# One fused attention and feed-forward kernel: the order of every engine's queue is made anew, and some operations change engine

## The chip, the cores and the metric

The kernel runs on one core of one Trainium2 chip. A time is the device time of one execution in microseconds (us). The profile shows one execution: its span is the time from the first to the last instruction that the hardware profiler recorded. The engines are named as in the profile: PE (TensorE, with PEld for its weight loads), DVE (VectorE), ACT (ScalarE), POOL (GpSimd) and SP (SyncE, which here only issues transfers). L12 is line 12 of the kernel.

## The reference

The program first computes a routed attention and then a feed-forward layer on its result. Tokens attend only to tokens of the same cluster; the cluster is the centroid that lies nearest by angle.

```python
q_assign = np.argmax(np.einsum('bhsd,hcd->bhsc', q_n, c_n), axis=-1)
k_assign = np.argmax(np.einsum('bhsd,hcd->bhsc', k_n, c_n), axis=-1)
mask = q_assign[:, :, :, None] == k_assign[:, :, None, :]
scores = np.where(mask, scale * np.matmul(q, k.transpose(0, 1, 3, 2)), -1e9)
attn = np.exp(scores - np.max(scores, axis=-1, keepdims=True))
x = np.matmul(attn / (np.sum(attn, axis=-1, keepdims=True) + 1e-09), v)
# then, on tokens x (head, dim):
h = x @ w_in
solu = h * softmax(h)
out = ((solu - mean(solu)) / sqrt(var(solu) + 1e-06) * g_ln) @ w_out
```

There are 4 batches of 8 heads with 768 tokens of 64 numbers, 16 centroids for each head, and a feed-forward layer from 512 to 1024 to 512 over the 3072 tokens. All inputs and the output are float32.

## The kernel before

**Work and stages.** Heads are taken in pairs, 16 pairs in all (batch.pair, as in 0.3). For each pair, queries and keys are loaded (ld on SP), turned so that the head's dimension lies on the partitions, and cast to bf16 into a tile qk. In batch 0 the turning is done on PE (tp, L391 and L395) with copies out of PSUM (xa, L405, on ACT or DVE); in the other batches it is a transpose on DVE (xt, L419). The casts are called ca (L443 on ACT, L445 for queries and L447 for keys on POOL or DVE). The cluster of each token comes from a matmul against the centroids (cl, L457 or L462), a transpose back on DVE (tb, L471), a maximum over 16 columns (mx, L484), a comparison with it that makes a one-hot row (oh, L489), another transpose (ot, L495), and four copies of it beside the queries and keys (pl, L507 or L514, on POOL or DVE, or as a transfer, L512). A small memset (bl, L523) blanks the columns that belong to the other head. With the one-hot rows beside the data, one matmul gives scores that are shifted down wherever two clusters differ.

**Attention.** The scores of a pair go through PSUM banks of 512 columns: matmuls S (L593), the exponential E on ACT (L599), and the matmuls V (L616) that multiply by the values. The PSUM tile for the scores has 3 buffers, the exponentials have 9, the sums have one. N (L628 and L641, on DVE) divides by the denominators and writes x; the next group's V must wait for it. The values come by lv (SP) and a cast cv (L532).

**Feed-forward.** Tokens go in 24 blocks f of 128. For each there is a transposing transfer of x (tx, SP, L671; the last block on PE), matmuls h (L702), the maximum hm on DVE (L708), the exponential ex on ACT (L714), the product u on DVE (L721), a transposing transfer tu (SP, L726), statistics bn and ag on DVE (L732, L736), the scale factor at and al on POOL (L742 to L751), the output matmuls y (L768) and the scaling sc (L786 on ACT, L788 on DVE), and the store ou. h of the block after next, and part of the next, writes into the PSUM bank that u of block f has read. The output weights are loaded (lo), summed (su, L571, DVE), averaged by one matmul (me) and centred (ce, L579, DVE); the input weights are loaded (li) and cast (wi, L551, POOL).

**What sets the order.** Each of these operations is registered under its name. A table ORDER holds one string for each engine: it lists kinds of operations, and the k-th entry of a kind takes the k-th registered operation of that kind on that engine. A table AWAY names the operations that leave their usual engine. An engine works through its instructions in this order and stops at one whose inputs are not there. The tables were written out by a search ahead of time; the kernel itself does no search.

## Time and profile before

| what | value |
| --- | --- |
| median of 3 runs | 228.95 us (228.57 to 230.77) |
| the profiled execution, its own time | 228.39 us |
| its span | 226.4 us |
| PE busy | 218.4 us, 96% |
| DVE busy | 200.4 us, 89%, 353 instructions |
| ACT busy | 194.7 us, 86%, 378 instructions |
| POOL busy | 132.9 us, 59%, 256 instructions |
| moved by DMA | 39.00 MB, mean 172 GB/s |

The profiled execution took 2.0 us more than its span, and lies 0.56 us below the median. A busy share is an average over stages: the first 60 us are attention alone with all preparations of the first batch and of the weights, from about 55 to 205 us attention and feed-forward run side by side, and the last 20 us are feed-forward alone. An engine's row in the profile gives busy time, number of instructions and mean duration of one; instructions of one engine can overlap a little, so a sum of durations is more than the engine's busy time.

### The profile page before, as it was taken

To read this page: it belongs to the slowest core of one execution; us is meant where nothing else is said; L and a number is where in the kernel's file an instruction comes from. 1 tells how busy PE (TensorE), PEld (TensorE's weight loads), DVE (VectorE), ACT (ScalarE), POOL (GpSimd) and SP (SyncE) were. 2 spreads that over 40 slices of the span, in tenths; PEclk is the share of its full clock that TensorE was granted. 3 is DMA by queue.
4 is the path that set the end of the run, shared out by engine and by line. 5 is a ranking of instruction groups with operands and counts; after the bars stand their busy time and mean duration, and the time that the engine had idled before them with its cause. 6 is when DMAs were issued, how large, how long until landed. Compare 5 with 4: busy or idle time off the path is not lost.

```text
span 226.4 us, 6687 instructions
## 1 busy us (share of the span) xinstructions
PE 218.4 (96%) x2460; PEld 148.7 (66%) x2460; DVE 200.4 (89%) x353; ACT 194.7 (86%) x378; POOL 132.9 (59%) x256
## 2 busy tenths in 40 slices
PE   7899988999999999999999999999999999999993
PEld 4566655666777767686577767687677677675452
DVE  3699999999999899999999989899899969798991
ACT  3689979999999999999889999899999999974352
POOL 4577799982498589387949742485908403223311
PEclk9999999999999999999999999999999999999999
DMA  6996988699998999999998949579924441476922
GB/s 154 343 353 163 258 226 120 256 157 252 149 172 147 248 229 181 146 166 163 185 232 144 215 101 210 126 161 210 243 59 110 97 116 26 61 150 181 186 86 106
DMA packets 123183, 39.00 MB, mean 172 GB/s; under 512 B 112008, under 2 KB 117904, under 8 KB 123152
## 3 DMA queue, kind: packets, MB, share of 16 engines
q1 hardware_dynamic: 122432, 38.06, 79.5%
q10 hardware_dynamic: 720, 0.52, 0.8%
q8 instruction: 19, 0.31, 0.6%
q14 instruction: 12, 0.10, 0.1%
HBM read 23.11 MB, written 6.29 MB: 130 GB/s over the span
## 4 chain that ended last, share of the span: by engine, by line
PE 74%; DMA 8%; DVE 8%; SPq 7%; issue 1%; ACT 0%; DVEq 0%
PE sps L593 22%; PE hreg L702 18%; PE yps L768 17%; PE ops L616 13%; SPq L411 4%; PE csc L462 3%; DMA w_g<-in_moe_w_out_dram 3%; DMA w_st<-in_moe_w_in_dram 2%; DVE w_out_c L579 2%; DMA raw<-in_k_dram 2%; DVE xt L419 1%; SPq L564 1%; DMA raw<-in_q_dram 1%; PE hreg L768 1%; SPq L376 1%
## 5 line engine op out<-in xcount | busy, mean ns | idle before, releaser
L599 ACT ACTIVATE e<-sps 128x512 bf16<-128x512 f32 (+1 forms) x294 | 151.8, 595 | 11.9 <-PE sps L593 10.1
L593 PE MATMUL sps<-qk 96*128 96x256 bf16 (+5 forms) x636 | 93.3, 264 | 2.1 <-DVE qk L507 0.6
L593 PEld LDWEIGHTS <-qk 96*128 96x128 bf16 (+1 forms) x636 | 59.5, 121 | 27.1 <-issue 7.6
L616 PEld LDWEIGHTS <-e 128*128 128x128 bf16 x1152 | 49.7, 97 | 12.1 <-issue 3.1
L616 PE MATMUL ops<-v,e 128*128 128x65 bf16 x1152 | 54.2, 193 | 0.6 <-DVE x L641 0.5
L702 PE MATMUL hreg<-w_in_sb,xT 128*128 128x512 bf16 x192 | 52.9, 379 | 0.3 <-DVE w_out_c L579 0.3
L768 PE MATMUL yps<-w_out_c,uT 128*128 128x512 bf16 x184 | 47.4, 378 | 0.0
L514 POOL COPY qk<-oht 32x384 f32<-32x384 f32 (+1 forms) x45 | 22.2, 493 | 19.5 <-DVE oht L495 17.1
L721 DVE TENSOR_TENSOR u<-e_sb,hreg 128x1024 bf16<-128x1024 bf16 (+1 forms) x25 | 29.1, 1169 | 2.8 <-ACT e_sb L714 2.5
L708 DVE TENSOR_REDUCE nmax<-hreg 128x1 f32<-128x1024 f32 x24 | 29.3, 1219 | 2.6 <-PE hreg L702 2.0
L732 DVE BATCH_NORM_STATS2 bs<-u 128x6 f32<-128x512 bf16 x48 | 31.2, 674 | 0.2
L714 ACT ACTIVATE e_sb<-hreg,nmax 128x1024 bf16<-128x1024 f32 x24 | 26.9, 1120 | 3.0 <-DVE nmax L708 2.9
L445 POOL CAST qk<-xt 64x768 bf16<-64x768 f32 (+1 forms) x32 | 26.5, 829 | 4.7 <-ACT xt L405 3.3
L447 POOL TENSOR_SCALAR qk<-xt 64x768 bf16<-64x768 f32 (+1 forms) x31 | 26.8, 864 | 2.2 <-DVE xt L405 0.2
L768 PEld LDWEIGHTS <-uT 128*128 128x128 bf16 x200 | 18.3, 97 | 14.2 <-ACT uT L698 0.5
L702 PEld LDWEIGHTS <-xT 128*128 128x128 bf16 x192 | 17.1, 97 | 10.0 <-DVE w_out_c L579 0.6
L419 DVE STREAM_TRANSPOSE xt<-raw 128x768 f32<-128x768 f32 x24 | 22.8, 958 | 0.0
L742 POOL TENSOR_SCALAR es<-esum 128x1 f32<-128x1 f32 x24 | 5.8, 246 | 27.1 <-ACT e_sb L714 26.5
L748 POOL TENSOR_SCALAR esq<-es,mv 128x1 f32<-128x1 f32 x24 | 8.3, 344 | 21.3 <-DVE mv L736 21.1
L641 DVE TENSOR_TENSOR x<-ops,den 128x256 bf16<-128x256 f32 (+1 forms) x39 | 19.0, 486 | 1.3
L532 POOL CAST v<-vf 128x384 bf16<-128x384 f32 x28 | 14.2, 522 | 5.9 <-DMA vf<-in_v_dram 4.5
L786 ACT ACTIVATE y<-yps,alpha 128x512 f32<-128x512 f32 x17 | 11.7, 690 | 6.6 <-PE yps L768 5.8
(79 smaller groups left out, 178.3 us busy)
## 6 DMA issues: line engine op xcount, KB each, us to landing
vf<-in_v_dram SPq DMA_DIRECT2D x16, 384.0 KB, 4.4
out_dram<-y SPq DMA_DIRECT2D x23, 256.0 KB, 2.7
raw<-in_q_dram SPq DMA_DIRECT2D x50, 96.0 KB, 3.1
raw<-in_k_dram SPq DMA_DIRECT2D x50, 96.0 KB, 3.2
w_g<-in_moe_w_out_dram SPq DMA_DIRECT2D x4, 512.0 KB, 7.2
w_st<-in_moe_w_in_dram SPq DMA_DIRECT2D x4, 512.0 KB, 5.3
raw<-in_q_dram SPq DMA_DIRECT2D x3, 384.0 KB, 6.6
raw<-in_k_dram SPq DMA_DIRECT2D x3, 384.0 KB, 7.0
```

The source lines that it names most:

```text
L419: nc.vector.transpose(xt[:], raws[b, p, i][:].rearrange("p j c -> p (j c)"))
L445: VEC[e].tensor_copy(dst, src)
L447: VEC[e].tensor_scalar(dst, src, scalar1=inv_C, scalar2=1.0, op0=Alu.mult, op1=Alu.mult)
L593: nc.tensor.matmul(sps_[n, k][:, c0:c0 + w], side(b, h // 2, 1, h % 2, keys)[r], side(b, h // 2, 0, h % 2, slice(s0 * P, s0 * P + w))[r])
L599: nc.scalar.activation(es[n, k][:, :w], sps_[n, k][:, :w], Act.Exp, scale=exp_scale, bias=-exp_scale)
L616: nc.tensor.matmul(opss[g][:, s, :VW], es[n, k][:, c0:c0 + P], v1[slot(b, h // 2)][:, h % 2, kt, :VW], start=(kt == 0), stop=(kt == n_t - 1))
L702: uses(nc.tensor.matmul(hreg[:, at(f, f2)[1], :], xTs[f][:, dc, :], w_in_sb[:, dc, f2 * FF2:(f2 + 1) * FF2], start=(dc == 0), stop=(dc == ...
L708: uses(nc.vector.tensor_reduce(ff[f, "nmax"][:], pair_of(f), axis=AXY, op=Alu.max, negate=True), *both(f))
L714: uses(nc.scalar.activation(ff[f, "e"][:], pair_of(f), Act.Exp, bias=ff[f, "nmax"][:], accum_out=ff[f, "esum"][:]), *both(f))
L721: uses(nc.vector.tensor_tensor(ff[f, "u"][:, r], ff[f, "e"][:, r], pair_of(f)[:, r], op=Alu.mult), *both(f)[r])
L732: nc.vector.bn_stats(ff[f, "bs"][:, f2, :], ff[f, "u"][:, f2, :])
L768: ins = nc.tensor.matmul(dst, ff[f, "uT"][:, at(f, f2)[0] * (n_fc // 2) + c, :], w_out_c[:, fc, cols], start=(fc == fcs[0] and part % 2 == ...
```

## The change

Both tables are replaced by new ones. The arithmetic, the tiles, the buffers and the set of operations stay as they were. The search that made the new tables took it as a rule that a DVE operation whose operands all lie in SBUF (it touches no PSUM) and a POOL operation cannot run at the same time; the search before had no such rule. What the tables say of the place of each operation changed nearly everywhere, so only one line of the order and the lists of operations moved to ACT and DVE are shown here.

```diff
     ORDER["DVE"] = """
-        cn cb tb mx oh ot pl3 tb mx oh ot xa2 cf ca2 bl tb mx oh gk ot N pl su xa su tb mx oh xa ot
+        cn cb ca tb mx oh ot pl2 tb mx oh ot pl xa2 cf ca cv pl tb mx xa oh gk ot N ca pl tb su mx
...
-        ca0.0.0.1.1 sc23.0 xa0.0.0.1 xa0.0.1.0 xa0.1.0.0 xa0.1.0.1 xa0.2.0.0 xa0.2.0.1 xa0.2.1.0
-        xa0.2.1.1 xa0.3.0.0
+        ca0.0.0.0.0 ca0.1.1.1 ca0.3.0.0 ca2.3.0.0 sc23.0 tu22.1 xa0.0.0.1 xa0.0.1.0 xa0.1.1.0
+        xa0.1.1.1 xa0.2.0.0 xa0.2.0.1 xa0.2.1.1
     """.split(), "ACT"))
     AWAY.update(dict.fromkeys("""
-        bl0.0.1 bl0.2 bl1.2 bl1.3 bl3.3 ca0.0.1.1.1 ca0.1.0.0 cv3.0.0 cv3.1.0 cv3.3.0 cv3.3.1
-        pl0.0.0.1.1 pl0.1.1.0 pl0.2.0.1 pl0.3.0.0 sc10 sc17 sc19 sc2 sc6 sc9 tu22.0
+        bl1.0 bl2.3 ca0.0.0.1.0 ca0.1.0.1 ca0.2.1.1 ca1.0.0.0 ca1.3.0.0 ca1.3.0.1 ca2.0.0.0
+        ca2.2.0.1 ca2.3.1.0 ca3.0.1.1 ca3.3.0.1 cv0.0.0 cv2.2.0 pl0.0.0.0.1 pl0.0.0.1.1 pl0.0.1.0.1
+        pl0.1.1.1 pl0.2.0.0 sc0 sc10 sc12 sc13 sc19 sc23.1 sc3 sc4 sc8 tu22.0
     """.split(), "DVE"))
```

By engine, these counts change: casts ca, on POOL 63 before and 49 now, on DVE 2 and 11 (one of each half-size), on ACT 3 and 8; scalings sc, on ACT 19 and 16, on DVE 6 and 9; copies xa, on DVE 5 and 7, on ACT 11 and 9; casts cv, on DVE 4 and 2; memsets bl, on DVE 5 and 2; copies tu, on DVE 3 and 2. The copies pl on DVE are 6 in both. The changed file has one line more in the SP table, so that every line number behind it is larger by one: L391 is L392, L445 is L446.

The first place is PE's queue at the program's start, behind the warming matmuls: the transposes tp0.0 of the first pair's four half loads (L391), the centroids' transpose cp (L866) and the first cluster matmuls cl0.0.0 (L462). Before:

```order
L391 MATMUL hreg<-ident_f,raw 64x128 x12
L866 MATMUL cps<-ident_f,c_n 128x128
L391 MATMUL hreg<-ident_f,raw 64x128 x6
L462 MATMUL csc<-xt,c_bd 32x192 x4
L391 MATMUL hreg<-ident_f,raw 64x128 x6
```

Now:

```order
L392 MATMUL hreg<-ident_f,raw 64x128 x12
L867 MATMUL cps<-ident_f,c_n 128x128
L463 MATMUL csc<-xt,c_bd 32x192 x4
L392 MATMUL hreg<-ident_f,raw 64x128 x12
L817 LDWEIGHTS w_out_c
```

The first cluster matmuls now stand ahead of the third group of transposes instead of behind it.

The second place is DVE's queue behind the second cluster assignment: xa (L405), cf (L870), casts ca (L445 and L447), a memset bl (L523) and the assignment of pair 0.1 (L471 to L495). Before:

```order
L405 COPY xt<-hreg 128x384 x2
L870 TENSOR_TENSOR w_out_c<-cps,w_out_c 128x512
L447 TENSOR_SCALAR qk_99<-xt 64x384
L445 CAST qk_100<-xt 64x6x128
L523 MEMSET qk_99 16x192
L471 STREAM_TRANSPOSE cst<-csc 128x384
L484 TENSOR_REDUCE mx<-cst 128x24
L489 TENSOR_TENSOR oh<-cst,mx 128x384
```

Now:

```order
L515 COPY qk_99<-oht 32x2x96
L406 COPY xt<-hreg 128x384 x2
L871 TENSOR_TENSOR w_out_c<-cps,w_out_c 128x512
L446 CAST qk_100<-xt 64x6x128
L533 CAST v_0_105<-vf 128x6x64
L515 COPY qk_99<-oht 32x2x96
L472 STREAM_TRANSPOSE cst<-csc 128x384
L485 TENSOR_REDUCE mx<-cst 128x24
L406 COPY xt<-hreg 128x384
L490 TENSOR_TENSOR oh<-cst,mx 128x384
```

A half-size cast and the memset left this stretch, and a cast of values, two copies pl and one more copy xa came into it.

The third place is DVE's queue around hm of block 4 (the row L708, or L709, below), in the stage where attention and feed-forward run side by side; bn and ag are L732 and L736, xt is L419. Before:

```order
L736 BN_AGGR mv<-bs 128x2
L419 STREAM_TRANSPOSE xt<-raw 128x768
L732 BN_STATS bs<-u 128x6 x2
L736 BN_AGGR mv<-bs 128x2
L788 TENSOR_SCALAR y<-yps,alpha 128x512
L708 TENSOR_REDUCE nmax<-hreg 128x1
L628 RECIPROCAL den<-ops 128x4
```

Now:

```order
L420 STREAM_TRANSPOSE xt<-raw 128x768
L709 TENSOR_REDUCE nmax<-hreg 128x1
L446 CAST qk_100<-xt 64x768
L420 STREAM_TRANSPOSE xt<-raw 128x768
L446 CAST qk_100<-xt 64x768
L733 BN_STATS bs<-u 128x6
L629 RECIPROCAL den<-ops 128x6
L642 TENSOR_TENSOR x<-ops,den 128x6x64
```

Behind hm of block 4 stand two casts of queries that POOL did before, and a transpose between them.

## The prediction

> **What bounds the kernel now.** I read the page first for who is busy and when. In its second part each digit is the busy tenth of one fortieth of the span, 5.7 us.

> ```profile
> span 226.4 us, 6687 instructions
> ...
> PE   7899988999999999999999999999999999999993
> ...
> DVE  3699999999999899999999989899899969798991
> ...
> PE 74%; DMA 8%; DVE 8%; SPq 7%; issue 1%; ACT 0%; DVEq 0%
> ```

> PE is full from the tenth slice to the last but one, and the chain that ended last runs through it for 74% of the span. A new order cannot shorten work on a full engine, so a gain must come from the first 55 us or from the last few. The busy time by stretch shows who limits the beginning; the last two rows are the stage in which attention and feed-forward run side by side.

> ```profile
> core 0: us, PE busy (x) PEld busy (x) DVE busy (x) ACT busy (x) POOL busy (x), PEclk, DMA share, GB/s
> 10.00:20.00 10.00, 9.45 (x100) 6.38 (x98) 9.48 (x20) 8.96 (x24) 7.28 (x14) 1.00 1.02 310
> 20.00:30.00 10.00, 9.85 (x124) 6.20 (x122) 9.85 (x16) 8.61 (x20) 8.43 (x15) 1.00 0.84 213
> 30.00:40.00 10.00, 8.25 (x126) 5.45 (x123) 9.59 (x19) 9.00 (x18) 9.38 (x14) 1.00 0.85 171
> 40.00:50.00 10.00, 9.75 (x129) 6.65 (x126) 9.80 (x20) 9.70 (x21) 9.48 (x16) 1.00 0.90 202
> 50.00:60.00 10.00, 9.66 (x117) 7.00 (x116) 9.73 (x16) 9.36 (x19) 3.99 (x8) 1.00 1.00 212
> ...
> 57.80:117.40 59.60, 59.60 (x695) 42.66 (x694) 56.46 (x95) 57.06 (x110) 42.48 (x77) 1.00 1.01 183
> 117.40:216.00 98.60, 98.56 (x1093) 67.38 (x1091) 88.65 (x149) 84.81 (x160) 46.50 (x93) 1.00 0.70 142
> ```

> From 10 to 60 us DVE is the fullest engine: of 50 us it is idle for 10.00 − 9.48 and so on, 1.55 us in all, while PE misses 3.0 us and ACT 4.4. DVE sets the pace there, up to the maximum hm of block 1 at 57.8 us. Between 57.8 and 117.4 us PE is busy for all 59.60 us, DVE idle for 59.60 − 56.46 = 3.1. Between 117.4 and 216 DVE is idle for 98.60 − 88.65 = 10.0.

> **What a collision costs.** The groups by shape and the durations (least, median, most, in ns) of single lines tell which DVE operations lengthen beside POOL.

> ```profile
> L489 DVE TENSOR_TENSOR oh<-cst,mx x17: 516/698/1267, 8.6 to 168.5; 128x384 bf16<-128x384 f32 x15, 128x192 bf16<-128x192 f32 x2
> L571 DVE SCALAR_TENSOR_TENSOR w_sum<-w_g,g_ln,w_sum x7: 703/741/1193, 21.8 to 39.4; 128x512 f32<-128x512 f32 x7
> L507 DVE COPY qk<-oht x3: 473/881/886, 20.0 to 37.2; 32x384 f32<-32x384 f32 x3
> L732 DVE BATCH_NORM_STATS2 bs<-u x48: 637/679/696, 59.8 to 220.3; 128x6 f32<-128x512 bf16 x48
> L419 DVE STREAM_TRANSPOSE xt<-raw x24: 924/968/978, 27.6 to 156.5; 128x768 f32<-128x768 f32 x24
> ...
> 41.65 1.27 DVE L489 TENSOR_TENSOR oh<-cst,mx 128x384 bf16<-128x384 f32 x1
> ...
> 41.47 2.35 POOL L551 CAST w_in_sb<-w_st 128x1024 bf16<-128x1024 f32 x2
> ...
> 5.00:60.00 55.00, 6.25 (x7) 1.00 0.92 230
> ```

> The longest oh, 1.27 us at 41.65, started beside a cast that POOL had begun at 41.47; alone an oh takes 0.52. The statistics and transposes keep their durations within 60 ns, whatever POOL does. The last row is oh alone before 60 us. So in the first 60 us collisions took 6.25 − 7 × 0.516 = 2.6 us in oh, 7 × (0.837 − 0.703) = 0.9 in su (its mean is in the next rows), 0.88 + 0.89 − 2 × 0.47 = 0.8 in two copies pl, and up to 0.5 in one cast, **4.8 us in all**, on the engine that sets the pace.

> **The change part by part.** Durations for what moves:

> ```profile
> L571 DVE SCALAR_TENSOR_TENSOR w_sum<-w_g,g_ln,w_sum 128x512 f32<-128x512 f32 x7 | 5.9, 837 | 0.0
> L788 DVE TENSOR_SCALAR y<-yps,alpha 128x512 f32<-128x512 f32 x6 | 4.5, 746 | 1.3 <-issue 0.8 <-PE yps L768 0.6
> L405 DVE COPY xt<-hreg 128x384 f32<-128x384 f32 x5 | 2.6, 539 | 0.0
> L523 DVE MEMSET qk<- 16x384 f32 x4 | 1.5, 378 | 0.5
> L532 DVE CAST v<-vf 128x384 bf16<-128x384 f32 x4 | 1.3, 351 | 0.0
> L445 DVE CAST qk<-xt 64x768 bf16<-64x768 f32 x1 | 1.1, 1077 | 0.0
> L443 ACT ACTIVATE qk<-xt 64x384 bf16<-64x384 f32 x3 | 1.5, 517 | 0.0
> L405 ACT COPY xt<-hreg 128x384 f32<-128x384 f32 x11 | 5.2, 507 | 3.0 <-PE hreg L391 3.0
> ```

> A full cast on DVE is measured once, 1.08 us, beside POOL. Below, it cannot be less than the cast of half as many columns, 0.35; twice that is 0.70 with the fixed part counted double. I take 0.60 undisturbed and keep 0.35 and 1.08 as ends.

> Start. DVE waits 1.60 us for the first cluster matmuls:

> ```profile
> 5.85 0.29 DVE L876 TENSOR_TENSOR c_bd<-cps,own 128x128 f32<-128x128 f32 x1 [0.71 <-PE cps L866]
> 7.75 0.38 DVE L471 STREAM_TRANSPOSE cst<-csc 128x192 f32<-128x192 f32 x1 [1.60 <-PE csc L462]
> ...
> 6.35 0.87 PE L391 MATMUL hreg<-ident_f,raw 128*64 128x128 f32 x10 [0.17 <-DMA raw<-in_q_dram]
> 7.15 0.53 PE L462 MATMUL csc<-xt,c_bd 128*32 128x192 f32 x8
> ```

> They now stand ahead of the transposes that run from 6.35 with a wait for a load; the wait shortens by some 0.9 us. The half-size cast set ahead of it on DVE (0.5) fits into the 0.7 us left: **−0.9 us**.

> Collisions up to 57.8 us. I take two thirds as avoided, **−3.2**: POOL is rid of 14 casts and the order keeps the pairs apart, but the engines drift against a plan, and every collision avoided must hold on the chip. Ends: 0 and −4.8.

> DVE's added work up to hm of block 1: by the order's rows, two full casts (1.2), two copies xa (1.1), a cast of values (0.35) and less memset (−0.2): **+2.4** (1.9 with casts at 0.35, 3.4 at 1.08). ACT, with 4.4 us idle in this stage, gets two full casts (at most twice 0.52 each) and two half-size ones and gives up two copies xa, +2.1 us, and stays below DVE. Loads hardly shift the limit: the last input weights come behind the same set of transfers, though lo2 and lo3, which feed su, come behind eight small loads now; su5 to su7 stand later on DVE, too.

> Side by side, 57.8 to 117.4 us. DVE gets four full casts (2.4), a cast of values (0.35), two scalings sc (1.5) and two memsets less (−0.8): +3.5 us, against 3.1 of idle time. That idle time is made of waits for h and ex within the loop of a block (h, hm, ex, u, then the next h into the bank), so I count half as usable, 1.6, and 0.5 of collisions of oh gone: **+1.4**. Ends: 0, if all of it is usable; 3.5 or more, if none. PE has no idle time here, so what DVE is late, PE loses for good.

> From 117.4 to 216 us three more casts (1.8) stand against four casts of values fewer (−1.4), with 10 us idle: 0.

> Tail. The chain of the end runs through u, the statistics, DVE's copy of u and the last output matmuls:

> ```profile
> 219.80 1.21 DVE bs L732 x2
> ...
> 221.58 1.50 PE hreg L768 x12
> ...
> 218.67 0.69 ACT L786 ACTIVATE y<-yps,alpha 128x512 f32<-128x512 f32 x1 [0.19 <-POOL esq L748]
> 220.14 0.59 ACT L698 COPY uT<-utp 128x512 bf16<-128x512 bf16 x1 [0.78 <-PE utp L690]
> ```

> The statistics stay ahead of the copy. ACT gets one more copy (tu22.1, 0.59) between these two rows, where it has 0.78 idle, and y22 waits for it: **+0.2** (−0.2 to +0.6).

> Sum: −0.9 − 3.2 + 2.4 + 1.4 + 0.2 = −0.1 us. The profiled execution, 226.4 of span and 2.0 around it, would become 228.3; the median lies 0.56 above, so 228.8 us.

> [...]

> **The rivals.**
> 1. *The collisions go entirely, and DVE's idle time is usable.* −0.9 − 4.8 + 2.4 + 0 + 0.2 = −3.1: 225.8 us. For it: POOL loses work. Against it: ACT had only 0.3 us idle between 40 and 50, so the gain must be made before.
> 2. *The moved casts collide and DVE becomes the bound* (slower). Each of nine full casts at 1.08 instead of 0.60: the start gives −0.9 − 1.6 (a third avoided) + 3.4 = +0.9; side by side 4 × 1.08 + 0.35 + 1.5 − 0.8 = 5.4, less 1.6, is +3.8; with the tail +4.9: 233.8 us. It decides once DVE's extra work between 57.8 and 117.4 us passes its 3.1 us of idle time. For it: PE is without a gap there. Against it: POOL's queue is shorter, so a cast on DVE meets less.
> 3. *The change doesn't do what it says.* A plan that keeps xt and bn apart from POOL as well spends its freedom on pairs that cost nothing, and on the chip oh and su still collide: a third avoided (−1.6), half a microsecond more lost side by side: −0.9 − 1.6 + 2.4 + 1.9 + 0.2 = +2.0: 231.0 us.

> **How the numbers follow.** About 1%, 2.3 us, is what a measurement here tells from no change: faster means below 226.7, slower above 231.2. The forecast has 0.48, the rivals 0.20, 0.16 and 0.16. Of the forecast's spread 0.04 falls on each side; the third rival lies half inside 1%. That gives faster 0.24, same 0.40 + 0.08 = 0.48, slower 0.04 + 0.16 + 0.08 = 0.28. The range reaches down to the first rival and up past the third, 225.7 to 231.8; the second is left out.

> **What would show it.** The first DVE transpose of clusters would start near 6.8 us instead of 7.75; oh before 60 us would sum to about 4.5 instead of 6.25; hm of block 1 would start near 56. DVE casts near 0.6 speak for the forecast, near 1.0 for the second rival. PE's busy time between 57 and 118 us below the stretch's length, with waits for N or u, would show DVE as the bound. I am wrong if PE shows gaps after 120 us, or if the beginning is held by loads: su or wi waiting for its transfer.

## The result, and the profile after

The changed kernel takes **228.69 us** (median of 20 executions, 227.94 to 229.42), the kernel before 229.00 us in the same comparison (20 executions, 227.90 to 232.96). The ratio is 0.9992 with a 95% interval of 0.9972 to 1.0011: no change that can be measured. The prediction was 228.8 us, with no change as its likeliest case. The time came out as the sum said, but three of the sum's terms did not, and their errors cancelled.

| | before | after |
| --- | --- | --- |
| the profiled execution, its own time | 228.39 us | 229.03 us |
| its span | 226.4 us | 227.1 us |
| centroids' transpose (cp) starts, on PE | 5.49 us | 6.45 us |
| hm of block 1 starts | 57.76 us | 58.44 us |
| hm of block 23 starts | 216.01 us | 216.49 us |

The page of the kernel after: the length of the span, two rows of busy tenths, and the shares of the chain that ended last.

```profile
span 227.1 us, 6660 instructions
...
PE   7999978999999999999999999999999999999993
...
DVE  2699999999999999999999999998999589798991
...
PE 82%; DVE 10%; DMA 2%; issue 2%; POOL 1%; ACT 1%; SPq 0%; DVEq 0%; ACTq 0%
```

PE is full from the eighth slice on, as in the row of before (the prediction reads that row as full from the tenth), and its share of the chain went from 74% to 82%. PE still has emptier places in the sixth and seventh slice, from 28 to 40 us. The busy times by stretch, of the kernel after, for the same stretches as those shown of before:

```profile
core 0: us, PE busy (x) PEld busy (x) DVE busy (x) ACT busy (x) POOL busy (x), PEclk, DMA share, GB/s
10.00:20.00 10.00, 9.96 (x113) 6.57 (x111) 9.20 (x20) 9.39 (x24) 5.85 (x13) 1.00 1.11 310
20.00:30.00 10.00, 9.84 (x125) 6.46 (x118) 9.72 (x18) 9.18 (x20) 6.31 (x13) 1.00 0.81 142
30.00:40.00 10.00, 8.25 (x118) 5.59 (x117) 9.78 (x18) 9.09 (x19) 8.04 (x17) 1.00 1.05 317
40.00:50.00 10.00, 9.55 (x122) 6.40 (x120) 9.46 (x20) 9.28 (x20) 4.94 (x6) 1.00 0.60 138
50.00:60.00 10.00, 9.62 (x116) 7.33 (x117) 9.67 (x17) 9.94 (x21) 6.33 (x11) 1.00 0.87 162
57.80:117.40 59.60, 58.97 (x695) 43.20 (x706) 58.11 (x98) 57.05 (x111) 40.17 (x73) 1.00 1.03 179
```

From 10 to 60 us POOL is busy for 31.5 us instead of 38.6, DVE for 47.8 instead of 48.5: the work that left POOL is there, but DVE's time hardly fell. From 30 to 40 us PE is busy for 8.25 us, as before. Side by side, DVE's busy time went from 56.46 to 58.11 us. (In the trace of after 17 records of h are missing, so its PE rows from 57.8 us on read a little low.)

Where DVE's time went, in the kernel after. The first row is oh alone before 60 us (the second number is its busy time), then come groups by shape, the durations (least, median, most, in ns) of two lines' instructions on DVE, and single instructions from the timeline (start, duration):

```profile
5.00:60.00 55.00, 4.12 (x7) 1.00 0.89 222
...
L572 DVE SCALAR_TENSOR_TENSOR w_sum<-w_g,g_ln,w_sum 128x512 f32<-128x512 f32 x7 | 5.7, 815 | 0.1
L508 DVE COPY qk<-oht 32x384 f32<-32x384 f32 x2 | 1.5, 745 | 0.0
L406 DVE COPY xt<-hreg 128x384 f32<-128x384 f32 x7 | 3.6, 544 | 0.3 <-PE hreg L396 0.2
...
L446 DVE CAST qk<-xt x8: 354/555/1086, 7.1 to 164.7; 64x768 bf16<-64x768 f32 x7, 64x384 bf16<-64x384 f32 x1
L533 DVE CAST v<-vf x2: 555/716/878, 15.1 to 100.2; 128x384 bf16<-128x384 f32 x2
...
13.94 1.09 DVE L446 CAST qk<-xt 64x768 bf16<-64x768 f32 x1
15.06 0.88 DVE L533 CAST v<-vf 128x384 bf16<-128x384 f32 x1
20.05 0.84 DVE L448 TENSOR_SCALAR qk<-xt 64x768 bf16<-64x768 f32 x1
```

oh before 60 us fell from 6.25 to 4.12 us. With the rows of su (0.2 less) and of the copies pl (from 3.5 to 2.7 us, in part because one of the six is half as large now) DVE spends 3.1 us less on these three, about what the forecast had said. But the casts that came to DVE are long themselves: 1.09, 0.84 and 0.88 us, where the same shapes also appear at 0.55.

One thing has to be known before any two spans are compared. PE starts this program at half its speed: the first transposes, in pairs, come every 0.21 us and later every 0.11. How long the 24 first ones take on PE, behind the same warming matmuls, shows when that ends (rows of the timeline of before, then of after):

```profile
3.84 1.72 PE L391 MATMUL hreg<-ident_f,raw 128*64 128x128 f32 x24
5.49 0.33 PE L866 MATMUL cps<-ident_f,c_n 128*128 128x128 f32 x1
```

```profile
3.85 2.68 PE L392 MATMUL hreg<-ident_f,raw 128*64 128x128 f32 x24
6.45 0.33 PE L867 MATMUL cps<-ident_f,c_n 128*128 128x128 f32 x1
```

They took 1.72 us in the profiled execution of before and 2.68 us in that of after. The experiments show that this differs from execution to execution; so times below are also counted from cp, which stands right behind these transposes.

### The profile page after: what moved, and what is told of

The parts are those of the page before. It is cut to its first block, busy times and chain, and to the rows that moved or that the text cites. A ratio compares the mean times of both kernels' runs of the same rounds, so it can differ in the third digit from the quotient of the medians.

```text
span 227.1 us, 6660 instructions
## 1 busy us (share of the span) xinstructions
PE 217.4 (96%) x2429; PEld 150.1 (66%) x2460; DVE 203.8 (90%) x361; ACT 195.9 (86%) x379; POOL 122.0 (54%) x246
## 4 chain that ended last, share of the span: by engine, by line
PE 82%; DVE 10%; DMA 2%; issue 2%; POOL 1%; ACT 1%; SPq 0%; DVEq 0%; ACTq 0%
PE sps L594 24%; PE hreg L703 18%; PE yps L769 16%; PE ops L617 13%; PE csc L463 4%; DMA raw<-in_k_dram 2%; PE hreg L392 2%; DVE w_sum L572 2%; PE idle_p L817 2%; PE hreg L396 1%; DVE xt L420 1%; DVE oht L496 1%; DVE oh L490 1%; POOL v L533 1%; DVE cst L472 1%
## 5 line engine op out<-in xcount | busy, mean ns | idle before, releaser
L594 PE MATMUL sps<-qk 96*128 96x256 bf16 (+5 forms) x636 | 94.5, 264 | 1.6 <-ACT e L600 1.0
L594 PEld LDWEIGHTS <-qk 96*128 96x128 bf16 (+1 forms) x636 | 60.8, 121 | 29.8 <-issue 9.5
L703 PE MATMUL hreg<-w_in_sb,xT 128*128 128x512 bf16 x175 | 48.8, 379 | 0.9
L515 POOL COPY qk<-oht 32x384 f32<-32x384 f32 (+1 forms) x43 | 21.7, 504 | 32.3 <-DVE oht L496 30.5
L709 DVE TENSOR_REDUCE nmax<-hreg 128x1 f32<-128x1024 f32 x24 | 29.1, 1213 | 2.8 <-PE hreg L703 2.5
L769 PEld LDWEIGHTS <-uT 128*128 128x128 bf16 x200 | 17.8, 97 | 10.6 <-DVE uT L697 0.8
L448 POOL TENSOR_SCALAR qk<-xt 64x768 bf16<-64x768 f32 x26 | 22.4, 860 | 2.7 <-DVE xt L420 1.4
L446 POOL CAST qk<-xt 64x768 bf16<-64x768 f32 (+1 forms) x23 | 18.4, 801 | 7.0 <-ACT xt L406 6.1
L533 POOL CAST v<-vf 128x384 bf16<-128x384 f32 x30 | 15.5, 527 | 1.7 <-DMA vf<-in_v_dram 0.7
L787 ACT ACTIVATE y<-yps,alpha 128x512 f32<-128x512 f32 x15 | 10.3, 687 | 5.6 <-PE yps L769 4.1
L752 POOL TENSOR_TENSOR alpha<-esq,halves 128x1 f32<-128x1 f32 x24 | 13.4, 560 | 2.0
```

The costliest lines, as they stand in the source:

```text
L448: VEC[e].tensor_scalar(dst, src, scalar1=inv_C, scalar2=1.0, op0=Alu.mult, op1=Alu.mult)
L515: ins = VEC[e].tensor_copy(dst.bitcast(F32), src.bitcast(F32).unsqueeze(1) .to_broadcast([NB, 2, n // 2]))
L594: nc.tensor.matmul(sps_[n, k][:, c0:c0 + w], side(b, h // 2, 1, h % 2, keys)[r], side(b, h // 2, 0, h % 2, slice(s0 * P, s0 * P + w))[r])
L703: uses(nc.tensor.matmul(hreg[:, at(f, f2)[1], :], xTs[f][:, dc, :], w_in_sb[:, dc, f2 * FF2:(f2 + 1) * FF2], start=(dc == 0), stop=(dc == ...
L709: uses(nc.vector.tensor_reduce(ff[f, "nmax"][:], pair_of(f), axis=AXY, op=Alu.max, negate=True), *both(f))
L769: ins = nc.tensor.matmul(dst, ff[f, "uT"][:, at(f, f2)[0] * (n_fc // 2) + c, :], w_out_c[:, fc, cols], start=(fc == fcs[0] and part % 2 == ...
```

## The experiments

**1. Which DVE operations lose time beside POOL.** The kernel after with a piece appended behind its work: each DVE form twice alone, twice beside a stream of POOL casts, twice beside a stream of POOL memsets. Only the appended part is read.

```diff
+    forms()                                        # each form alone
+    for _ in range(26):
+        nc.gpsimd.tensor_copy(qk[1][:D, :S], qk[2][:].bitcast(F32)[:D, :S])
+    forms()                                        # beside POOL casts
+    for _ in range(40):
+        nc.gpsimd.memset(qk[1][:NC_, :768].bitcast(F32), 0.0)
+    forms()                                        # beside POOL memsets
```

> The changed kernel with DVE forms measured by themselves behind its work: two each of the comparison (as oh), the sum of weights (as su), a cast of 64x768, a copy of 32x384, a transpose (as xt), a maximum (as mx), statistics (as bn) and a memset, first with POOL idle, then beside an unbroken row of POOL casts of 64x768, then beside an unbroken row of POOL memsets. The appended part makes the program some 60 us longer and its time says nothing. My theory (only DVE operations with two SBUF inputs, and copies and casts, collide with POOL): beside casts oh goes from 0.52 to 0.9 to 1.3 us, su from 0.70 to 1.1 to 1.5, cast and copy rise by 0.4 to 0.8; transpose, maximum, statistics and memset stay within 0.06 us. Rival (the rule of the search: every DVE operation on SBUF alone collides): all eight rise by 0.4 us or more. [...]

The durations of the oh form (least, median, most), then rows of the timeline, each for two instructions (start, time of the two): su, cast, transpose and statistics, alone from 225 us, beside casts from 237, beside memsets from 262 us.

```profile
L1232 DVE TENSOR_TENSOR qk<-w_g x6: 548/558/1060, 224.2 to 262.0; 128x384 bf16<-128x384 f32 x6
...
225.40 1.54 DVE L1236 SCALAR_TENSOR_TENSOR qk<-w_g,g_ln 128x512 f32<-128x512 f32 x2
226.97 1.14 DVE L1240 CAST qk<-w_g 64x768 bf16<-64x768 f32 x2
228.91 1.99 DVE L1244 STREAM_TRANSPOSE qk<-w_g 128x768 f32<-128x768 f32 x2
...
232.11 1.42 DVE L1249 BATCH_NORM_STATS2 qk<-w_g 128x6 f32<-128x512 f32 x2
...
237.92 2.42 DVE L1236 SCALAR_TENSOR_TENSOR qk<-w_g,g_ln 128x512 f32<-128x512 f32 x2
240.37 2.15 DVE L1240 CAST qk<-w_g 64x768 bf16<-64x768 f32 x2
244.35 1.99 DVE L1244 STREAM_TRANSPOSE qk<-w_g 128x768 f32<-128x768 f32 x2
...
247.55 1.42 DVE L1249 BATCH_NORM_STATS2 qk<-w_g 128x6 f32<-128x512 f32 x2
...
262.61 1.54 DVE L1236 SCALAR_TENSOR_TENSOR qk<-w_g,g_ln 128x512 f32<-128x512 f32 x2
264.19 1.61 DVE L1240 CAST qk<-w_g 64x768 bf16<-64x768 f32 x2
```

Beside POOL casts a pair of su went from 1.54 to 2.42 us, a pair of casts from 1.14 to 2.15; the transposes stayed at 1.99 and the statistics at 1.42. In the same timeline pairs of the copy of 32x384 went from 0.73 to 1.75, those of the maximum and of the memset stayed at 1.14 and 0.89. Beside POOL memsets su stayed, the casts went to 1.61 and the copies to 1.10. So the theory holds, and its rival is out. The search's rule, that anything of DVE on SBUF alone excludes POOL, is thus too broad: it keeps transposes and statistics apart from POOL for nothing.

**2. The start: four operations given back to POOL.** The kernel after, with three full casts and a cast of values back on POOL; for this ca0.2.1.0, already on POOL, has to move ahead in POOL's queue as well.

```diff
+    AWAY.update({"cv0.0.0": "POOL", "ca0.1.0.1": "POOL", "ca0.2.1.1": "POOL", "ca1.0.0.0": "POOL"})
     ORDER["DVE"]
-        ... oh ot pl xa2 cf ca cv pl tb mx xa oh gk ot N ca pl tb su mx ... ce3 N ca ce2 hm
+        ... oh ot pl xa2 cf pl tb mx xa oh gk ot N pl tb su mx ... ce3 N ce2 hm
     ORDER["POOL"]
-        ca pl2 bl pl2 ca bl ca3 cv pl3 bl ca pl2 z cv2 pl z cv ca z3 sg cv
+        ca pl2 bl cv pl2 ca bl ca4 cv pl3 bl ca3 pl2 z cv2 pl z cv z3 sg cv
```

> The changed kernel with four DVE operations of the first 52 us given back to POOL, which has gaps there: the casts ca0.1.0.1, ca0.2.1.1, ca1.0.0.0 and the cast of values cv0.0.0. Theory (DVE sets the pace up to hm of block 1, as the prediction had it): about 2.5 us of DVE work goes, hm of block 1 comes 2 us earlier than in the changed kernel, and the time falls by 1.5 to 2.5 us, to about 226.5. Rival (the beginning is paced by several engines in turn, attention's E chain on ACT above all, and DVE work is only one of them): hm of block 1 moves by less than 0.7 us and the time by less than 0.7.

Measured: 227.01 us (11 executions, 226.43 to 227.63), ratio to before 0.9895 (0.9859 to 0.9930). cp and hm of block 1 in this kernel, and hm in the kernel after:

```profile
6.54 0.33 PE L868 MATMUL cps<-ident_f,c_n 128*128 128x128 f32 x1
...
56.81 1.19 DVE L710 TENSOR_REDUCE nmax<-hreg 128x1 f32<-128x1024 f32 x1
```

```profile
58.44 1.18 DVE L709 TENSOR_REDUCE nmax<-hreg 128x1 f32<-128x1024 f32 x1
...
216.49 1.22 DVE L709 TENSOR_REDUCE nmax<-hreg 128x1 f32<-128x1024 f32 x1
```

From cp to hm of block 1 it is 56.81 − 6.54 = 50.27 us against 58.44 − 6.45 = 51.99: the whole gain, 1.7 us, is made there, as large as the theory had it, and the rival is out. The first three of the four moved operations had taken 2.81 us of DVE, the fourth 0.75; 12 shows which of them counted.

**3. Side by side: four casts given back to POOL.** The kernel after with ca1.3.0.0, ca1.3.0.1, ca2.0.0.0 and ca2.2.0.1 on POOL, all between 57 and 117 us.

```diff
+    AWAY.update({"ca1.3.0.0": "POOL", "ca1.3.0.1": "POOL", "ca2.0.0.0": "POOL", "ca2.2.0.1": "POOL"})
```

> The changed kernel with the four DVE casts between hm of block 1 and hm of block 8 (ca1.3.0.0, ca1.3.0.1, ca2.0.0.0, ca2.2.0.1) given back to POOL. Theory of the prediction (side by side, DVE's added work cost PE 1.4 us): 2.0 us of DVE work goes and the time falls by about 1.4 us. Rival (the order placed PE work that waits for nothing behind the places where DVE is late, so nothing was lost): the time stays within 0.5 us, DVE's idle time between those two points grows by 1.5 to 2 us.

Measured: 228.82 us (12 executions), ratio 0.9973 (0.9937 to 1.0009); beside the 228.69 of the kernel after, no gain. hm of blocks 1 and 23:

```profile
58.56 1.18 DVE L710 TENSOR_REDUCE nmax<-hreg 128x1 f32<-128x1024 f32 x1
...
216.61 1.22 DVE L710 TENSOR_REDUCE nmax<-hreg 128x1 f32<-128x1024 f32 x1
```

It is 158.05 us between them, in the kernel after also 216.49 − 58.44 = 158.05. The casts on DVE cost nothing there; the rival is right.

**4. Side by side: 2.7 us more on DVE.** The kernel after with four statistics that nobody reads, behind u of blocks 2, 4, 6 and 7.

```diff
+    spare_st = const.tile([P, 6], F32, name="spare_st")
+    for j in range(4):
+        add(f"dm{j}", "DVE", 0.65, 0, lambda e: nc.vector.bn_stats(spare_st[:], w_g[:, 0, :]), ["lo0"])
```

> The changed kernel with four more statistics operations on DVE (their result is not used), about 0.67 us each, 2.7 us in all, behind u of blocks 2, 4, 6 and 7. They do not collide with POOL. Theory (DVE is at its bound there: 1.2 us of idle time is left between hm of block 1 and hm of block 8): the time rises by 1.5 to 2.7 us. Rival (what DVE is late is made up behind block 8, where DVE has 8 us of idle time and PE's order has work in hand): less than 0.7 us.

Measured: 229.97 us (12 executions), ratio 1.0033 (1.0001 to 1.0066). hm of blocks 1 and 23:

```profile
58.68 1.18 DVE L709 TENSOR_REDUCE nmax<-hreg 128x1 f32<-128x1024 f32 x1
...
218.07 1.22 DVE L709 TENSOR_REDUCE nmax<-hreg 128x1 f32<-128x1024 f32 x1
```

159.39 us between them, 1.34 more than after, between the theory and its rival: half of the 2.7 us is paid. So DVE has room for what the change gave it, and for about 1.4 us more, and what goes beyond that is paid. The mechanism of the prediction is there, only its threshold was set too low.

**5. The place of the first cluster matmuls, alone.** The kernel before with cl0.0.0 ahead of the third group of transposes.

```diff
-        wm tp2 cp tp cl tp fl4 cl fl tp2 S3
+        wm tp2 cp cl tp2 fl4 cl fl tp2 S3
```

> The kernel before with one edit in PE's queue at the start: the first cluster matmuls (the row of L462) stand ahead of the third group of transposes instead of behind it. In the profile before, the first transpose of clusters on DVE began 2.26 us after the centroids' transpose on PE, in the profile after 1.39 us. Theory (the start is on the path, as the prediction has it): that distance falls to about 1.4 us, hm of block 1 starts 0.9 us earlier if DVE sets the pace of the first 57 us, and the median falls by 0.5 to 0.9 us; and since the kernel before shows two groups of times, about 228.0 to 229.0 and 229.9 to 231.1, while the changed one shows 227.9 to 229.4 alone, the upper group goes if the third group of transposes, slow before PE's clock is up, is its cause. Rival (the start is covered by what follows): the distance falls, but hm of block 1 and both groups of times stay where they were.

Measured: 228.53 us (12 executions, 227.96 to 231.19), ratio 1.0009 (0.9960 to 1.0058). From cp to the first transpose of clusters it is 8.03 − 6.64 = 1.39 us, as forecast, and the time does not move; both groups of times remain, four of the twelve in the upper one. The ratio's interval alone would leave room for 0.9 us, but within the lower group it is 228.27 us (8 executions) against 228.36 (21 executions of before beside them). The theory fell, for the time and for the groups. But the profiled execution was one of the upper group, and it showed what that group is: the granted clock.

```profile
core 0: us, PE busy (x) PEld busy (x) DVE busy (x) ACT busy (x) POOL busy (x), PEclk, DMA share, GB/s
30.33:33.74 3.41, 2.30 (x34) 1.27 (x31) 3.14 (x8) 3.12 (x7) 3.16 (x6) 1.00 0.93 168
33.74:37.15 3.41, 3.40 (x28) 1.90 (x28) 2.69 (x5) 2.42 (x5) 3.18 (x7) 0.50 1.05 185
```

For 3.4 us from 33.7 us on PE had a clock of 0.50, behind 3.4 us in which it had been busy for 2.30, 67%.

**6. The start: 2.0 us more on DVE.** As in 4, three statistics behind the first, second and fourth N.

```diff
+    for j in range(3):
+        add(f"dm{j}", "DVE", 0.65, 0, lambda e: nc.vector.bn_stats(spare_st[:], w_g[:, 0, :]), ["lo0"])
```

> The changed kernel with three more statistics on DVE (0.65 to 0.69 us each, 2.0 us in all, results not used) behind the first, second and fourth N after the start, in the stretch up to hm of block 1. Theory (DVE sets the pace there, nothing of its time is spare): hm of block 1 starts 1.7 to 2.0 us later and the median rises by 1.5 to 2.0 us, to about 230.3. Rival (PE or ACT sets the pace and DVE has slack): the rise is below 0.7 us.

Measured: 229.74 us (12 executions), 1.05 more than the kernel after, between the two theories. The reading is not clean: in 11 of the 12 executions the mean granted clock was 0.990 to 0.993, as in the upper group of before, and the profile has the same piece at 0.50, from 34.1 to 37.5 us. It stands right behind 3.41 us in which PE was busy for 1.97 (58%); in the kernel after the emptiest such stretch has 2.30. From cp to hm of block 1 it is 53.12 us, 1.13 more than after.

**7. Both stretches relieved.** The edits of 2 and 3 together.

```diff
+    AWAY.update({"cv0.0.0": "POOL", "ca0.1.0.1": "POOL", "ca0.2.1.1": "POOL", "ca1.0.0.0": "POOL",
+                 "ca1.3.0.0": "POOL", "ca1.3.0.1": "POOL", "ca2.0.0.0": "POOL", "ca2.2.0.1": "POOL"})
```

> The changed kernel with eight operations given back from DVE to POOL: the four of the start that gave 227.0 us, and the four casts between 57 and 117 us that gave 228.8 us alone. Theory (after the start is relieved PE is full, and DVE has room between 57 and 117 us): no more than the start's own gain, 226.8 to 227.2 us. Rival (with the start relieved, DVE becomes the bound between 57 and 117 us): up to 1 us better than that, 226.0 to 226.5.

Measured: 227.50 us (12 executions, 226.26 to 228.10), ratio 0.9929 (0.9891 to 0.9967). No better than the start's relief alone (0.3 us above the theory's range), so the rival is out; its profiled span is 225.4 us, that of 2 225.3.

**8. The kernel before, a second profile.** No edit.

> The kernel before, unchanged, for one more profile of it. In its first profile the pairs of transposes on PE came every 0.21 us until 4.2 us and every 0.11 us from then on; in the profiles of the changed kernel and of three variants of it the spacing fell only between 6.0 and 6.4 us, behind the same warming matmuls. Theory (the moment differs from execution to execution and has nothing to do with the order): another profile of the same kernel can show any moment between, and a late one goes with a later first transpose of clusters and with a time of the upper group, about 230 to 231. Rival (the order decides it): it shows 4.2 us again.

Measured: 228.37 us, span 226.4, and the spacing of the transposes fell at 4.2 us again. Alone this would speak for the rival. But swap_only has the same instructions on PE until cp, and there it fell only behind 6.0 us; before_fill, below, has them too, and shows 5.7 us; and two variants of the changed kernel that differ in nothing before cp show 6.4 (start_back) and 3.9 us (start_unswap). So the moment belongs to the execution, not to the order. That a late one goes with the upper group did not come true: before_fill has one at 228.55 us. What it is worth can be read from these last two: cp at 6.54 and at 5.31 us, spans of 225.3 and 224.1, 1.2 us both.

**9. One of PE's gaps filled.** The kernel before with two matmuls on zeros ahead of S of unit 9, where PE would wait; S overwrites their result.

```diff
+        if (n, k) == (9, 0):
+            for _ in range(2):
+                nc.tensor.matmul(sps_[n, k][:], idle_w[:, :P], idle_w)
```

> The kernel before with two matmuls of 512 columns on zeros (about 0.43 us, results overwritten) ahead of S of unit 9, where PE waits 0.56 us for a memset on DVE, at 32.7 us. Executions of the kernel before fall into two groups: 38 of 57 with a granted clock of 0.998 or more, at 228.4 us, and 19 with a clock of 0.991 to 0.993, at 230.8. In the two profiles that showed such a clock it stood at 0.50 for 3.4 us, right behind a stretch of 3.4 us in which PE was busy for about two thirds. In the kernel before only a stretch that holds both of PE's gaps, at 31.4 and at 32.7 us, is as empty. Theory (the idle stretch lowers the clock, and how often depends on where the clock's windows fall): with one of the two gaps filled the lower clock is gone, none or one of about 12 executions, and the upper group with it; the rest stays at 228.2 to 228.6 us. Rival (the lower clock has another cause): about 4 of 12 still show it.

Measured: 228.52 us (12 executions, 228.01 to 229.30), all with a clock of 0.999 or more, while 9 of the 26 executions of the kernel before beside it were at 0.993 or less. The emptiest 3.4 us of before, then of this kernel, by stretch (the first busy time is PE's):

```profile
29.80:33.21 3.41, 2.29 (x35) 1.27 (x32) 3.14 (x8) 3.12 (x7) 3.16 (x6) 1.00 1.04 276
```

```profile
30.00:33.41 3.41, 2.52 (x36) 1.47 (x35) 3.14 (x8) 3.12 (x7) 3.16 (x6) 1.00 0.95 234
```

With 74% instead of 67% the lower clock is gone. Useless work on PE made the upper group vanish, at no cost to the rest (the other executions of before beside it have 228.41 us): the theory holds. From this kernel comes also the comparison that the two first profiles don't allow, an execution of before's order with a late cp and the full clock:

```profile
6.27 0.33 PE L869 MATMUL cps<-ident_f,c_n 128*128 128x128 f32 x1
...
58.22 1.21 DVE L711 TENSOR_REDUCE nmax<-hreg 128x1 f32<-128x1024 f32 x1
```

From cp to hm of block 1 it is 51.95 us, in the profiles of before 57.76 − 5.49 = 52.27 and, in the second, 57.56 − 5.48 = 52.08, in that of after 51.99.

**10. The first cluster matmuls put back, with the start relieved.** The kernel of 2 with cl0.0.0 behind the third group of transposes.

```diff
-        wm tp2 cp cl tp2 fl3 cl fl2 S2 cq
+        wm tp2 cp tp cl tp fl3 cl fl2 S2 cq
```

> The changed kernel with the four operations of the start on POOL (227.0 us), and the first cluster matmuls behind the third group of transposes again, as in the kernel before. In that kernel the chain of the end runs through PE alone from 5 to 28 us. Theory (the first cluster matmuls' place pays only where the chain begins there): the time rises by 0.5 to 0.9 us, to 227.5 to 227.9. Rival (the place is worth nothing in either kernel, since PE has the same work to do): 226.8 to 227.2.

Measured: 226.98 us (11 executions, 226.15 to 227.62), ratio 0.9911 (0.9878 to 0.9944), beside 227.01 with the changed place.

```profile
5.31 0.33 PE L868 MATMUL cps<-ident_f,c_n 128*128 128x128 f32 x1
...
55.59 1.18 DVE L710 TENSOR_REDUCE nmax<-hreg 128x1 f32<-128x1024 f32 x1
```

From cp to hm of block 1 it is 50.28 us, with the changed place 50.27. The rival is right: the place of the first cluster matmuls is worth nothing, in either kernel. The second transpose of clusters starts 3.88 us behind cp here, 3.95 with the changed place: what the first half gains does not reach the second, and the scores need both.

**11. One more cast from ACT to POOL.** The kernel of 2 with ca0.3.0.0 on POOL.

```diff
+    AWAY.update({..., "ca0.3.0.0": "POOL"})
```

> The changed kernel with the four operations of the start on POOL (227.0 us), and one more full cast of the start, of pair 0.3, given from ACT to POOL. ACT takes 0.84 us for it at 27.7 us and runs without a gap from 26.6 to 35 us there, and PE waits for its exponentials. Theory (with DVE relieved ACT sets the pace of that stretch): 0.3 to 0.8 us less, 226.2 to 226.7. Rival (PE sets it): no change, 226.8 to 227.2.

Measured: 227.25 us (10 executions, 226.40 to 227.86), ratio 0.9919 (0.9882 to 0.9955), no gain over 227.01. ACT does not set the pace there.

**12. One cast of the four alone.** The kernel after with ca0.2.1.1 on POOL; ca0.2.1.0 moves ahead with it.

```diff
+    AWAY.update({"ca0.2.1.1": "POOL"})
     ORDER["DVE"]
-        ... gk ot N ca pl tb su mx xa2
+        ... gk ot N pl tb su mx xa2
     ORDER["POOL"]
-        ... pl3 bl ca pl2 z cv2 pl z cv ca z3 sg cv
+        ... pl3 bl ca3 pl2 z cv2 pl z cv z3 sg cv
```

> The changed kernel with one of the four operations of the start alone on POOL: the second cast of the keys of pair 0.2, which takes 0.84 us on DVE at 20.05 us. Counted from the centroids' transpose on PE, hm of block 1 starts 51.99 us later in the changed kernel and 50.27 us later with all four on POOL; the two kernels go apart between 13 and 28 us after that transpose, and the two operations that stand ahead of that (1.09 and 0.88 us) leave DVE idle for 1.36 us when they are gone. Theory (behind the first N DVE's time counts in full, and this cast carries most of it): that distance falls to 50.4 to 50.9 us and the median to 227.1 to 227.6 us. Rival (the four count alike): about a quarter of the gain, 51.5 us and 228.2 us or more.

Measured: 227.17 us (12 executions, 226.44 to 227.91), ratio 0.9904 (0.9863 to 0.9946).

```profile
6.36 0.33 PE L868 MATMUL cps<-ident_f,c_n 128*128 128x128 f32 x1
...
56.65 1.19 DVE L710 TENSOR_REDUCE nmax<-hreg 128x1 f32<-128x1024 f32 x1
```

50.29 us from cp to hm of block 1: this one edit makes the whole gain of all four, more than the theory had given it, and 1.7 us is twice what the cast takes. The kernel after shows where. Rows of its DVE, POOL and PE, and of PEld's waits from 24 to 42 us:

```profile
30.34 0.93 DVE L508 COPY qk<-oht 32x384 f32<-32x384 f32 x1
...
29.93 0.82 POOL L448 TENSOR_SCALAR qk<-xt 64x768 bf16<-64x768 f32 x1
...
31.42 0.38 PE L594 MATMUL sps<-qk 80*128 80x256 bf16 x2 [0.79 <-ACT e L600]
...
38.56 0.55 PE L617 MATMUL ops<-v,e 128*128 128x65 bf16 x12 [0.47 <-DVE x L642]
...
PEld L594 <- POOL qk L448: 1.0, 1, 1.0
```

The copy in this variant:

```profile
29.42 0.35 DVE L509 COPY qk<-oht 32x384 f32<-32x384 f32 x1
```

S of unit 8, at 31.42 us, is the first on pair 0.2. It needs two things: the POOL row, which is ca0.2.1.0, placed behind copies and casts of values until 29.93, and the DVE row, the last copy pl of that pair, which comes late behind the cast of 20.05 us and, started beside the POOL row, takes 0.93 us. The copy ends last, at 31.27 us, the POOL row at 30.75. (The 0.79 us are put down to an exponential; ACT was done with it at 30.89 us by its own row.) In the variant the copy starts 0.83 us earlier, counted from cp, which is the time of the cast, and ends 1.4 us earlier; S of unit 8 starts 23.98 us behind cp instead of 24.97. That is 1.0 us of the 1.7. Most of the rest is the row at 38.56: V waits 0.47 us there for N on DVE, a wait that the variant does not have. From 24 to 60 us PE's waits sum to 2.1 us in the kernel after and to 0.5 in the variant. The edit moves the cast off DVE and ca0.2.1.0 ahead on POOL at once; which share each has was not taken apart. The kernels of 2, 10 and 12, all near 227.0 us, lie 1.5 to 1.7 us (0.7%) below the kernel after and about 1% below the kernel before (0.6% below its executions at the full clock, 228.42 us).

## Why the prediction was right, and where its steps failed

*Start, −0.9 us.* The wait ahead of the first transpose of clusters shortened as said (from 2.26 to 1.39 us behind cp), but "**the wait shortens by some 0.9 us**" is worth nothing at the end: experiments 5 and 10 show the same time with and without the move. The failed step is to count a first half that comes earlier without asking when the second half is there. The forecast "near 6.8 us" for that row was wrong for another reason, too: 7.84 us was measured, since PE was slow until 6.2 us in that execution.

*Collisions, −3.2 us.* Right in size: 3.1 us less in oh, su and pl, of which about 2.5 are collisions by the prediction's own prices. *DVE's added work, +2.4 us.* Too small: "**I take 0.60 undisturbed**" failed, the three full casts took 1.09, 0.84 and 0.75 us, the cast of values 0.88 instead of 0.35. Less the cast of 1.08 us that the kernel before had there, all casts of queries and keys add 1.45 us; with xa (+1.1 as forecast), the values and the memset (−0.2) the sum is 3.2. These casts lie between the forecast's 0.60 and the second rival's 1.08; side by side and later they took 0.55 to 0.6, as the forecast has it.

*The ramp as a whole, −1.7 us.* From cp to hm of block 1 after takes 51.99 us, before 51.95 to 52.27 in three profiles: 0.0 to −0.3. The two terms above account for most of that: without the start, and with 3.2 for the added work, the prediction's own sum is −3.1 + 3.2 = +0.1, and DVE's busy time between the two rows is 48.9 us after and 48.6 before. So this comparison does not contradict the step "**DVE sets the pace there**". The experiments limit it: one_back has 46.9 us of DVE's time in this stretch, 2.0 less than after, and takes 1.7 us less; start_back has 44.7, 4.2 less, and takes no less than one_back (50.27 against 50.29). A microsecond on DVE thus did not count once wherever it stood. How far DVE is ahead of before depends on the row, too: at the assignment of pair 0.2 it is 2 us, counted from cp (21.50 − 6.45 = 15.05 against 22.60 − 5.49 = 17.11 us), with some 2.3 us of xa and sums of weights ahead of that row before and behind it now; at S of unit 8 it is 0.1 us (24.97 against 30.54 − 5.49 = 25.05), and 1.1 us with the edit of 12. Busy shares show which engine is nearly full; they do not show which of its instructions somebody waits for.

*Side by side, +1.4 us.* Measured 0: hm of block 1 to hm of block 23 takes 158.05 us after, 216.01 − 57.76 = 158.25 before. The term was mis-sized, "**half as usable**" should have been all of it: from hm of block 1 to hm of block 8 DVE's work grew by 3.6 us (3.5 forecast) and its idle time fell from 3.1 to 1.6 us. PE lost nothing by it: in one_back, which has the same work there and a trace without gaps in its records, PE is busy for all 61.69 us of that stretch. Experiment 4 finds a price only behind another 1.4 us.

*117.4 to 216 us: 0, and the tail: +0.2.* Nothing measured speaks against either; from hm of block 23 to the end it is 10.4 us before and 10.6 after (10.3 to 10.4 in other profiles of before's order, 10.4 to 10.8 in those of after's).

So −1.7 became about 0 and +1.4 became 0. That the errors had opposite signs is luck. The rivals: the first needed usable idle time side by side, and had it, but not the gain at the start; the second had the direction of the casts' price at the start, but not its size, and had the price side by side wrong; the third, 231.0 us, is out.

The median of before hides something else. Of 100 executions of it beside the experiments 65 had a mean granted clock of 0.998 or more, with a median of 228.42 us, and 35 one of 0.993 or less, with 230.92. All 20 executions of the changed kernel had 0.999 or more. By these medians, taken on several chips, the changed kernel is 0.3 us slower where both have the full clock, and 2.2 us faster where the kernel before loses it. Nothing in the prediction spoke of that, and the median of 229.00 us against 228.69 shows neither.

## What to carry to other kernels

A near-full engine is not a path: before time is added up on it, find the next instruction of another engine that waits, and count only what stands ahead of that; here one cast taken off DVE, with another moved ahead on POOL, was worth 1.7 us, and three more operations taken off, with 2.2 us of DVE's time, nothing on top. Where a constraint is put into a planner, measure it form by form first: this rule was too broad, and casts that came to DVE with it took up to 1.09 us; that a finer rule gives a faster kernel was not run. Where executions of one kernel fall into two groups, look at the granted clock by stretch before anything else.
